# Chunked attention and mixer on one Trainium2 core: all weight factors split from joined words, stores issued from ScalarE's queue, and five pieces of batch 1's attention one border later

## The chip, the cores and the metric

The kernel runs on one core of a Trainium2 chip. The metric is the device time of one execution in microseconds; the time before is the median of three runs. A profile of one execution shows where that execution spent its time.

## The reference, cut to what matters

```python
# q, k, v: (B=4, H=8, S=768, D=64); mem_k, mem_v: (4, 8, 8, 64)
for c in range(24):                       # chunks of 32 queries
    keys = 8 memory keys + positions 32c-16 .. 32c+40 (cut at the ends)
    out[chunk] = softmax(q_c @ keys.T / 8) @ values
x = out, heads side by side               # (4, 768, 512)
h = x.transpose(0, 2, 1) @ U @ V          # U (768, 32), V (32, 768)
u = x + h.transpose(0, 2, 1)
result = u + relu(u @ w1) @ w2            # w1 (512, 2048), w2 (2048, 512)
```

U, V, w1 and w2 arrive as 64-bit numbers. The kernel reads each as two 32-bit words and joins them into one 32-bit number before use.

## The kernel before, in words

Every large product is made of float32 numbers split into a high and a low part, so one product of the mathematics is three products on TensorE. The work of one core goes in this order.

*Batch 0's attention* comes first, in an order written by hand. *Batch 0's mixer* follows in `both_blocks` (L1190): 32 units, each a `w1_step` (L1118, 12 matmuls of 384 columns on one slice f of 128 columns of w1, then ReLU and its split into `hh` and `hl`) and a `w2_step` (L1147, 9 matmuls of 512 columns). Units 0 to 17 take slices 0 to 8 for both blocks of 384 tokens; units 18 to 24 are slices 9 to 15 of block 0, units 25 to 31 the same of block 1. During these units the weights are loaded (raw words `rw`, `raw`), joined and split. `Words` (L197) joins: two ScalarE passes (L217, L231), two VectorE passes (L224, L225) and a VectorE addition (L238). `finish` (L363) issues the store of the joined slice to `val_d` from GpSimd's queue (L366) and makes the low half `w1l` on VectorE (L374) in one of the four buffers of the pool `wlo`. `save_w1l` (L339) is called with the next slice and issues from SyncE's queue (SP): for slices from 9 on `w1l` itself (L343), and for every slice half of `w1h` and half of `w1l`, 128 KB each, to `half_d` (L346).

*Attention of batch 1* is put between the units from 19 on: `border` (L1266) is called twice in each unit, before and after its `w1_step`, and lets the generator of the attention take as many steps as the next entry of `PLAN` (L48) says: transposes of k and q (L589), scores (`kall,qt`, L663), transposes of the probabilities (`ident,pt`, L748), weighing with v (`vb,pT`, L766), and at its end the mixing over tokens (L1004, and six matmuls `g,v` at L1028, each into a bank that VectorE then adds to x, L1030). What is left at unit 28 is done by `following`, which then calls `fold_both` (transposes L1307, VectorE folds L1317 and splits L1322).

*Batches 1 to 3* use seven products in place of eight, after Strassen's scheme. Eight pairs p of w1 slices each have seven factors (`PRODUCTS`, L51), each a tile of high and low halves. `prepare` (L1276) loads two joined slices of `val_d` and has GpSimd make five sums. `build_factor` (L1348) turns a sum into a factor: a ScalarE cast (L1357) and a VectorE subtraction (L1358). Factors 1 and 3 are no sums; they are loaded whole from `half_d` (L1354), 256 KB each, 46 times from ScalarE's queue and twice from SP's. Pairs follow each other without a pause; the factors of the next pair are built while the products of this one run.

The results and the folded x are put in a list `held`; `let_go` (L1107) issues their stores (L1110) from SP's queue at the next border. SP's queue runs in the order in which the program is written, as do TensorE's and GpSimd's; VectorE's from unit 18 on and ScalarE's from unit 2 on are ordered by a scheduler. PSUM banks: three in `ps_a`, two in `ps_h`, three in `ps_o`.

Of the kernel before, what the change touches and what calls it, by code (L numbers as in the profile page):

```python
# [9 lines left out]
F32 = mybir.dt.float32  # L10
# [34 lines left out]
SOON = 8  # L45
RATEL = 3
RATES = 6
PLAN = [0, 1, 1, 1, 1, 1, 1, 1, 1, 1, 1, 1, 1, 1, 1, 1, 2, 1, 1, 1, 0, 0, 0, 0, 0, 0]  # L48
SUMS = ((0, 0, 0, 0, 1, "add"), (2, 0, 0, 1, 1, "add"), (4, 1, 0, 1, 1, "add"),
        (5, 0, 1, 1, 1, "subtract"), (6, 1, 0, 0, 0, "subtract"))  # L50
PRODUCTS = ((6, 0), (2, 1), (0, 2), (1, 0), (5, 1), (4, 2), (3, 0))  # L51
# [4 lines left out]
def chunk_attn_then_mixer_kernel(  # L56
# [13 lines left out]
    nc = tc.nc  # L70
# [262 lines left out]
                c.append(raw)  # L333

    val_d = [dram.tile([P, NCK, P], F32, name=f"vald{f}") for f in range(NF)]
    half_d = [dram.tile([P, NCK, P], F32R, name=f"halfd{f}") for f in range(NF)]
    unsaved = []

    def save_w1l():  # L339
        while unsaved:  # L340
            f, w1l = unsaved.pop(0)
            if f >= SPLIT:
                nc.sync.dma_start(out=w1l_d[f].bitcast(F32), in_=w1l.bitcast(F32))  # L343
            c = 2 * (f % 2)
            for n, w in enumerate((w1h[f], w1l)):
                nc.sync.dma_start(  # L346
                    out=half_d[f][:, 2 * n:2 * n + 2].bitcast(F32), in_=w[:, c:c + 2, :].bitcast(F32),
                )

    def homes(f, which):  # L350
        if which == 0:
# [752 lines left out]
    def put_by(b, t):  # L1104
        held.append((x_d[b, t], xs.pop((b, t))))

    def let_go():  # L1107
        while held:
            to, x = held.pop(0)
            nc.sync.dma_start(out=to, in_=x)  # L1110

    def recall(b, blk):
        for t in range(blk * TB, blk * TB + TB):
# [23 lines left out]
    def add_to_x(b, t, bank, last):  # L1137
        x = xs[(b, t)]
        nc.vector.tensor_tensor(out=x, in0=bank, in1=x, op=ALU.add)
        if last:  # L1140
            held.append((out[b, t * P:(t + 1) * P, :], xs.pop((b, t))))
            if b == B - 1:
                let_go()

    accs = {}

# [43 lines left out]
    def both_blocks(following):  # L1190
# [11 lines left out]
        for n, (blk, f, where, begins, ends) in enumerate(units):  # L1202
            while done[0] < min(2 * NF, 2 * f + 1 + (n > LATE)):
                advance(1)
                more_w()
            if n == 2:
                head.close()
            let_go()
            solo = n >= 2 * SPLIT
            if n == 2 * SPLIT:  # L1210
                paced.close()
            for blk_, m, *_ in units[n:n + AHEAD + 1]:
                if m >= SPLIT and blk_ == 1:
                    get_w1l(m)
            w1l = w1ls[f]
            if f >= SPLIT or blk == 1:
                del w1ls[f]
            if n == 2 * SPLIT - SOON:
                place(1)
            serve(RATEL if n < 2 * SPLIT else RATES)  # L1220
            if n > 2 * SPLIT:
                border()
            if n == 0:
                for c, g3 in rest[:2]:
                    join_uT1(turn_x1(c), c, g3)
            if n == len(units) - 1:
                for m in range(3):
                    build_factor(0, m, nc.sync)
            hid_ = w1_step(0, blk, f, w1l)
            if n == len(units) - 2:  # L1230
                prepare(0)
            if n == len(units) - 5:
                open_turned()
            if n == len(units) - 1:
                open_fast()
                for m in range(3, len(PRODUCTS)):
                    build_factor(0, m, nc.sync)
            if n == 0:
                decode(2, 4)
                for c, g3 in rest[2:]:  # L1240
                    join_uT1(turn_x1(c), c, g3)
                decode(1, 1)
                decode(2, 6)
                decode(1, 6)
                decode(3, 2)
            for _ in range(RATE + (3 < n < 12)):
                advance(1)
                more_w()
            if n > 2 * SPLIT:
                border()  # L1250
            if n >= len(units) - 4:
                following()
            prev.append((blk, f, where, begins, ends) + hid_)
            if solo or n % 2 == 0 or ends:
                while len(prev) > (not ends):
                    while done[0] < 2 * prev[0][1] + 2:
                        advance(1)
                        more_w()
                    w2_step(0, *prev.pop(0))
# [16 lines left out]
    def prepare(p):  # L1276

        whole = [slot([P, NCK, P], F32, "val") for _ in range(2)]
        for side in range(2):
            nc.sync.dma_start(out=whole[side], in_=val_d[2 * p + side])  # L1280
        for m, (n, fa, ca, fb, cb, op) in enumerate(SUMS):
            if m % 2 == 0:
                two = slot([P, 2, 2, P], F32, "sums")
# [61 lines left out]

    factors = {}

    def build_factor(p, n, eng=nc.scalar):  # L1348
        if n < WLO:
            s = wlo.tile([P, NCK, P], F32R, name="w1l")  # L1350
        else:
            s = fast_pools[0].tile([P, NCK, P], F32R, name="s", bufs=len(PRODUCTS) - WLO)
        if n in (1, 3):
            eng.dma_start(out=s.bitcast(F32), in_=half_d[2 * p + (n == 1)].bitcast(F32))  # L1354
        else:
            total = mixed.pop((p, n))
            nc.scalar.copy(out=s[:, 0:2], in_=total)  # L1357
            nc.vector.tensor_tensor(out=s[:, 2:4], in0=total, in1=s[:, 0:2].bitcast(F32), op=ALU.subtract)  # L1358
        factors[p, n] = s

    def split_hidden(src):
# [159 lines left out]
```

## Time and profile before

| | before |
|---|---|
| median of three runs | 660.78 us |
| the three runs | 658.46, 660.78, 665.66 us |
| the profiled execution | 662.22 us |
| its span in the trace | 660.4 us |
| TensorE busy, share of the span | 629.3 us, 95% |
| VectorE, ScalarE, GpSimd busy | 63%, 44%, 20% |
| moved by DMA | 95.76 MB |

The span is 1.8 us shorter than the execution's own time, which holds a start and an end that no engine shows. In a row of the timeline the first number is the start in us, the second the duration in us; then come engine, line, operation, output<-input, and in brackets how long the engine sat idle before it and what ended that. A letter q behind an engine's name means its queue, that is an instruction that issues a DMA. PE is TensorE, DVE VectorE, ACT ScalarE, POOL GpSimd.

### The profile page before, as it was taken

The page shows a single profiled execution, that of the slowest core. Times are in us where ns is not written, and L with a number is a line of the kernel's source. Part 1 is how long each engine was busy: PE and PEld are TensorE (multiplying, and loading weights), DVE is VectorE, ACT ScalarE, POOL GpSimd, SP SyncE. Part 2 cuts the span into 40 slices and gives each one's busy share as a digit, 9 for nine tenths or more (in the row PEclk, how much of TensorE's full clock was granted, in tenths as well). Part 3 has the DMA queues.
Part 4 walks back from the last instruction along what each step waited for, and adds up shares of the span by engine and source line. Part 5 has one row for each costly group of instructions (what it writes and reads, how often), then busy time and mean ns, then how long its engine had stood idle before and what let it go on. Part 6 is the DMA issues. An engine that isn't in the chain of part 4 may idle for free.

```text
span 660.4 us, 15683 instructions
## 1 busy us (share of the span) xinstructions
PE 629.3 (95%) x6196; PEld 551.2 (83%) x6198; DVE 414.0 (63%) x839; ACT 290.7 (44%) x724; POOL 129.9 (20%) x192
## 2 busy tenths in 40 slices
PE   8798998989989999999999999999999999999997
PEld 7567997969868989988898898988979889989986
DVE  4877978766535955756665953746746976336342
ACT  4566776575313445533333545533433633314221
POOL 4610000200000243212410222202420358000000
PEclk9999998999979999999999999999999999999999
DMA  8899896668253478632422658731421474202111
GB/s 208 186 294 321 258 259 212 169 196 269 76 125 108 134 228 202 175 89 66 114 65 79 201 168 199 199 88 36 122 88 45 163 252 142 70 0 65 33 49 48
DMA packets 133075, 95.76 MB, mean 145 GB/s; under 512 B 88586, under 2 KB 107786, under 8 KB 133002
## 3 DMA queue, kind: packets, MB, share of 16 engines
q1 hardware_dynamic: 125002, 78.37, 41.5%
q10 hardware_dynamic: 6624, 12.06, 6.1%
q0 software_dynamic: 1376, 4.33, 1.8%
q8 instruction: 49, 0.80, 0.5%
q14 instruction: 24, 0.20, 0.1%
HBM read 72.58 MB, written 21.23 MB: 142 GB/s over the span
## 4 chain that ended last, share of the span: by engine, by line
PE 76%; DVE 7%; DMA 7%; issue 5%; ACT 2%; SPq 2%; POOL 0%; DVEq 0%; POOLq 0%; ACTq 0%
PE ps_h L1389 18%; PE acc L1176 13%; PE ps_a L1389 7%; PE acc L1181 6%; PE ps_h L1176 5%; PE ps_h L1125 5%; PE ps_a L1176 3%; PE ps_h L1181 3%; PE ps_a L589 2%; PE ps_a L766 2%; DMA vb<-in_v_dram 2%; PE ps_a L663 2%; PE ps_a L748 2%; PE ps_a L1181 1%; PE ps_a L1307 1%
## 5 line engine op out<-in xcount | busy, mean ns | idle before, releaser
L1285 POOL TENSOR_TENSOR sums<-val 128x256 f32<-128x256 f32 x120 | 94.3, 819 | 270.9 <-DMA val<-vald 101.5
L1176 PE MATMUL acc<-w,hh 128*128 128x512 f32 x366 | 97.6, 401 | 1.0 <-DVE w L374 1.0
L1389 PE MATMUL ps_h<-th,w1l 128*128 128x384 f32 x288 | 83.4, 343 | 2.3 <-DVE part L1406 1.2
L1176 PEld LDWEIGHTS acc<-w,hh 128*128 128x128 f32 x366 | 67.2, 189 | 15.3 <-issue 1.5
L1389 PEld LDWEIGHTS ps_h<-th,w1l 128*128 128x128 f32 x288 | 52.8, 188 | 6.7 <-issue 2.6
L1365 DVE SCALAR_TENSOR_TENSOR hl<-kept,hh 128x384 fp32r<-128x384 f32 x48 | 28.5, 594 | 44.3 <-PE ps_a L1181 24.3
L1389 PE MATMUL ps_h<-th,s 128*128 128x384 f32 x192 | 52.9, 336 | 0.0
L1181 PE MATMUL acc<-w,hl 128*128 128x512 f32 x183 | 51.8, 391 | 0.0
L1364 ACT ACTIVATE hh<-kept 128x384 fp32r<-128x384 f32 x48 | 25.5, 532 | 58.3 <-PE ps_a L1176 38.1
L1389 PE MATMUL ps_h<-tl,w1l 128*128 128x384 f32 x144 | 48.4, 336 | 0.0
L1125 PE MATMUL ps_h<-uh,w1h 128*128 128x384 f32 x124 | 43.3, 355 | 3.1 <-DVE hl L1132 3.1
L1176 PE MATMUL ps_h<-w,hh 128*128 128x512 f32 x156 | 43.0, 397 | 0.0
L1125 PE MATMUL ps_h<-ul,w1h 128*128 128x384 f32 x124 | 42.3, 349 | 0.6 <-issue 0.6
L1181 PEld LDWEIGHTS acc<-w,hl 128*128 128x128 f32 x183 | 34.4, 188 | 7.5
L1176 PE MATMUL ps_a<-w,hh 128*128 128x512 f32 x132 | 37.9, 390 | 1.8 <-ACT hh L1131 1.8
L1395 ACT COPY part<-ps_h 128x384 f32<-128x384 f32 x24 | 11.5, 480 | 59.7 <-PE ps_h L1389 56.9
L1357 ACT CAST s<-sums 128x256 fp32r<-128x256 f32 x72 | 28.4, 414 | 17.5 <-PE ps_h L1389 13.9
L1358 DVE TENSOR_TENSOR w1l<-sums,w1l 128x256 fp32r<-128x256 f32 x48 | 22.9, 492 | 19.8 <-ACT w1l L1357 19.8
L1389 PEld LDWEIGHTS ps_h<-th,s 128*128 128x128 f32 x192 | 35.1, 187 | 0.0
L1365 DVE SCALAR_TENSOR_TENSOR hl<-ps_a,hh 128x384 fp32r<-128x384 f32 x24 | 13.4, 557 | 33.8 <-ACT hh L1364 33.8
L1358 DVE TENSOR_TENSOR s<-sums,s 128x256 fp32r<-128x256 f32 x72 | 33.8, 484 | 0.8 <-ACT s L1357 0.8
L1176 PEld LDWEIGHTS ps_h<-w,hh 128*128 128x128 f32 x156 | 28.4, 188 | 5.6
(274 smaller groups left out, 1373.8 us busy)
## 6 DMA issues: line engine op xcount, KB each, us to landing
val<-vald SPq DMA_DIRECT2D x48, 256.0 KB
w1l<-halfd ACTq DMA_DIRECT2D x46, 256.0 KB
rw<-in_moe_w_ch_dram SPq DMA_DIRECT2D x14, 512.0 KB
out_dram<-x SPq DMA_DIRECT2D x24, 256.0 KB
vb<-in_v_dram SPq DMA_DIRECT2D x56, 98.0 KB
raw<-in_moe_w_ch_dram SPq DMA_DIRECT2D x20, 256.0 KB
qn<-in_q_dram SPq DMA_DIRECT2D x36, 128.0 KB
xd<-x SPq DMA_DIRECT2D x18, 256.0 KB
```

The lines of the kernel that those rows point to most:

```text
L589: nc.tensor.transpose(out=psv[:, p, r, :], in_=half[:, r, 2 * p:2 * p + 2, :].rearrange("n h d -> n (h d)"), identity=ident,)
L663: nc.tensor.matmul(out=psv[s][CK * i:CK * i + CK, t, p % 2, p // 2, :], lhsT=qt[p // 2][rows, p % 2, NI * t + i, :], rhs=kall[rows, NB * ( ...
L748: nc.tensor.transpose(out=psv[:, j, :], in_=pt[:, P * j:P * j + P], identity=ident)
L1125: nc.tensor.matmul(out=ph[:, :TOK], lhsT=w[:, c, :], rhs=u[c], start=(m == 0), stop=(m + 1 == len(parts)),)
L1176: nc.tensor.matmul(out=acc[tt], lhsT=h[:, sl], rhs=w, start=(begins and m == 0), stop=False,)
L1181: nc.tensor.matmul(out=acc[tt], lhsT=hl[:, sl], rhs=w2h[f], start=False, stop=ends is not None)
L1285: nc.gpsimd.tensor_tensor(out=two[:, m % 2], in0=a, in1=b_, op=getattr(ALU, op))
L1357: nc.scalar.copy(out=s[:, 0:2], in_=total)
L1358: nc.vector.tensor_tensor(out=s[:, 2:4], in0=total, in1=s[:, 0:2].bitcast(F32), op=ALU.subtract)
L1364: nc.scalar.activation(out=hh, in_=src, func=AF.Relu)
L1365: nc.vector.scalar_tensor_tensor(out=hl, in0=src, scalar=0.0, in1=hh.bitcast(F32), op0=ALU.max, op1=ALU.subtract,)
L1389: nc.tensor.matmul(out=banks[at_], lhsT=w[:, wc, :], rhs=t[:, i, c, :], start=(n < 3 and m == 0), stop=(m + 1 == len(parts)), skip_group_c ...
```

## The change

It has four parts. (1) `half_d` is gone, with its 32 stores and its 48 loads. (2) Factors 1 and 3 are split like the other five, straight from the joined slices that `prepare` has loaded: one cast and one subtraction each. (3) `let_go` issues its stores from ScalarE's queue; only the last batch's six results stay with SP. (4) `PLAN` puts steps 1 to 5 of batch 1's attention one border later, catches up with a 2 at the seventh entry, and puts the steps from the former second 2 on one border later, the last into `following`.

```diff
-PLAN = [0, 1, 1, 1, 1, 1, 1, 1, 1, 1, 1, 1, 1, 1, 1, 1, 2, 1, 1, 1, 0, 0, 0, 0, 0, 0]
+PLAN = [0, 0, 1, 1, 1, 1, 2, 1, 1, 1, 1, 1, 1, 1, 1, 1, 1, 1, 1, 1, 0, 0, 0, 0, 0, 0]
@@ save_w1l
             if f >= SPLIT:
                 nc.sync.dma_start(out=w1l_d[f].bitcast(F32), in_=w1l.bitcast(F32))
-            c = 2 * (f % 2)
-            for n, w in enumerate((w1h[f], w1l)):
-                nc.sync.dma_start(
-                    out=half_d[f][:, 2 * n:2 * n + 2].bitcast(F32), in_=w[:, c:c + 2, :].bitcast(F32),
-                )
@@ let_go
-    def let_go():
+    def let_go(eng=nc.scalar):
         while held:
             to, x = held.pop(0)
-            nc.sync.dma_start(out=to, in_=x)
+            eng.dma_start(out=to, in_=x)
@@ add_to_x
             if b == B - 1:
-                let_go()
+                let_go(nc.sync)
@@ prepare
+        mixed[p, 1], mixed[p, 3] = whole[1][:, 2:4, :], whole[0][:, 0:2, :]
@@ build_factor
-        if n in (1, 3):
-            eng.dma_start(out=s.bitcast(F32), in_=half_d[2 * p + (n == 1)].bitcast(F32))
-        else:
-            total = mixed.pop((p, n))
-            nc.scalar.copy(out=s[:, 0:2], in_=total)
-            nc.vector.tensor_tensor(out=s[:, 2:4], in0=total, in1=s[:, 0:2].bitcast(F32), op=ALU.subtract)
+        total = mixed.pop((p, n))
+        nc.scalar.copy(out=s[:, 0:2], in_=total)
+        nc.vector.tensor_tensor(out=s[:, 2:4], in0=total, in1=s[:, 0:2].bitcast(F32), op=ALU.subtract)
```

Three places show how the order moves. The first is SP's queue at 160 to 182 us of the trace before; `vb_103` and `vb_102` are tiles of v for batch 1's attention, `w1ld` the stored low halves of w1, `out_dram` the results of block 0. Before:

```order
L429 DMA w1l<-w1ld_122 128x512
L552 DMA vb_103<-mv 8x8x256 x2
L570 DMA vb_103<-in_v_dram 56x8x64 x4
L1110 DMA out_dram<-x 128x512 x3
L429 DMA w1l<-w1ld_123 128x512
L570 DMA vb_103<-in_v_dram 56x8x64 x4
L570 DMA vb_102<-in_v_dram 56x7x64
```

After:

```order
L423 DMA w1l<-w1ld_122 128x512
L546 DMA vb_103<-mv 8x8x256 x2
L564 DMA vb_103<-in_v_dram 56x8x64 x4
L423 DMA w1l<-w1ld_123 128x512
L564 DMA vb_103<-in_v_dram 56x8x64 x4
L564 DMA vb_102<-in_v_dram 56x7x64
```

The three stores no longer stand between the two halves of `vb_103`; they now stand in ScalarE's queue.

The second place is TensorE at the scores of the first tile (unit 20 before, unit 21 after), where `ident,kn` and `ident,qn` are the transposes of k and q and `kall,qt` the scores. Before:

```order
L1125 MATMUL ps_h<-uh,w1l 128x384 x4
L589 MATMUL ps_a<-ident,kn 128x128 x8
L1176 MATMUL acc_1290<-w_1832,hh 128x512 x2
L1176 MATMUL acc_1291<-w_1832,hh 128x512 x2
L1176 MATMUL acc_1292<-w_1832,hh 128x512 x2
L1181 MATMUL acc_1290<-w_1832,hl 128x512
L1181 MATMUL acc_1291<-w_1832,hl 128x512
L1181 MATMUL acc_1292<-w_1832,hl 128x512
L663 MATMUL ps_a<-kall,qt 32x64 x64
```

After:

```order
L1119 MATMUL ps_h<-uh,w1l 128x384 x4
L657 MATMUL ps_a<-kall,qt 32x64 x64
L1170 MATMUL acc_1270<-w_1890,hh 128x512 x2
L1170 MATMUL acc_1271<-w_1890,hh 128x512 x2
L1170 MATMUL acc_1272<-w_1890,hh 128x512 x2
L1175 MATMUL acc_1270<-w_1890,hl 128x512
L1175 MATMUL acc_1271<-w_1890,hl 128x512
L1175 MATMUL acc_1272<-w_1890,hl 128x512
L583 MATMUL ps_a<-ident,kn 128x128 x8
```

The scores stood behind unit 20's nine matmuls with w2; now unit 21's w1 step comes first, and they stand ahead of its nine. The transposes of k have changed places with them in the same way: from behind a w1 step to behind the nine matmuls that followed it.

The third is TensorE in unit 28, the end of batch 1's attention, where `g,v` is the mixing over tokens and `ident,x` the first transposes of the fold. Before:

```order
L1028 MATMUL ps_a<-g_3023,v_99 128x512 x3
L1125 MATMUL ps_h<-uh_1133,w1h_1960 128x384
L1125 MATMUL ps_h<-ul_1134,w1h_1960 128x384
L1125 MATMUL ps_h<-uh_1133,w1h_1960 128x384
L1125 MATMUL ps_h<-ul_1134,w1h_1960 128x384
L1125 MATMUL ps_h<-uh_1133,w1h_1960 128x384
L1125 MATMUL ps_h<-ul_1134,w1h_1960 128x384
L1125 MATMUL ps_h<-uh_1133,w1h_1960 128x384
L1125 MATMUL ps_h<-ul_1134,w1h_1960 128x384
L1125 MATMUL ps_h<-uh_1133,w1l 128x384 x4
L1028 MATMUL ps_a<-g_3023,v_99 128x512 x3
L1307 MATMUL ps_a<-ident,x 128x128 x8
```

After:

```order
L1119 MATMUL ps_h<-ul_1118,w1h_1922 128x384
L1119 MATMUL ps_h<-uh_1117,w1h_1922 128x384
L1119 MATMUL ps_h<-ul_1118,w1h_1922 128x384
L1119 MATMUL ps_h<-uh_1117,w1l 128x384 x4
L1022 MATMUL ps_a<-g_2998,v_99 128x512 x6
L1302 MATMUL ps_a<-ident,x 128x128 x8
```

The w1 step that stood between the two groups of three now stands ahead of both.

## Rows read from the trace of the kernel before

**Rows 1.** The page's first part: busy time, share of the span, instructions of each engine.
```profile
PE 629.3 (95%) x6196; PEld 551.2 (83%) x6198; DVE 414.0 (63%) x839; ACT 290.7 (44%) x724; POOL 129.9 (20%) x192
```

**Rows 2.** Windows: start:end us, length, busy per engine, PEclk, DMA share, GB/s.
```profile
60.00:64.00 4.00, 4.00 (x21) 3.61 (x21) 3.90 (x8) 2.10 (x6) 0.00 (x0) 1.00 0.81 271
...
90.00:100.00 10.00, 10.00 (x52) 9.18 (x52) 6.81 (x13) 6.06 (x14) 0.78 (x1) 1.00 0.97 249
...
109.00:112.70 3.70, 3.70 (x14) 3.60 (x14) 3.70 (x8) 1.61 (x4) 0.54 (x1) 0.56 0.18 73
...
184.50:191.20 6.70, 6.08 (x94) 5.31 (x79) 1.85 (x7) 0.45 (x1) 0.00 (x0) 0.50 0.75 169
...
240.00:640.00 400.00, 396.54 (x3509) 352.38 (x3508) 236.87 (x483) 157.45 (x395) 90.52 (x122) 1.00 0.39 113
```

**Rows 3.** Timeline of POOL, DVE and PE, 92 to 109 us.
```profile
93.19 0.78 POOL L366 DMA_DIRECT2D vald<-vb  x1 [4.52 <-DVE vb L238]
...
99.39 0.43 DVE L224 TENSOR_SCALAR vb<-vb 128x512 int32<-128x512 int32 x1 [3.02 <-DMA vald<-vb]
...
108.76 0.44 PE L1125 MATMUL ps_h<-uh,w1h 128*128 128x384 f32 x1 [3.09 <-DVE hl L1132]
```

**Rows 4.** DMA issues of the whole run: KB each, median us to landing.
```profile
vald<-vb POOLq DMA_DIRECT2D x5, 256.0 KB, 4.0
```

**Rows 5.** Timeline of PE, 59 us: an earlier wait.
```profile
59.79 1.66 PE L1176 MATMUL ps_a<-w,hh 128*128 128x512 f32 x6 [1.77 <-ACT hh L1131]
```

**Rows 6.** Timeline of PE, 136 to 145 us.
```profile
136.12 0.66 PE L589 MATMUL ps_a<-ident,kn 128*128 128x128 f32 x4 [0.66 <-DVE x L1139]
137.32 0.66 PE L589 MATMUL ps_a<-ident,kn 128*128 128x128 f32 x4 [0.54 <-DVE x L1139]
...
144.76 0.66 PE L589 MATMUL ps_a<-ident,kn 128*128 128x128 f32 x4 [1.27 <-ACT kall L619]
```

**Rows 7.** Timeline of SP, DVE and PE, 176 to 183 us.
```profile
176.32 2.22 SPq L1110 DMA_DIRECT2D out_dram<-x  x3
...
179.07 2.84 SPq L570 DMA_DIRECT2D vb<-in_v_dram  x5
...
181.80 1.28 DVE L682 TENSOR_TENSOR pt<-ps_a,mx 128x512 f32<-128x512 f32 x2
...
180.20 0.27 PE L766 MATMUL ps_a<-vb,pT 64*32 64x64 f32 x2
182.93 0.35 PE L766 MATMUL ps_a<-vb,pT 64*32 64x64 f32 x16 [2.46 <-DMA vb<-in_v_dram]
```

**Rows 8.** Timeline of DVE and PE, 204 to 209 us.
```profile
204.57 1.89 DVE L1030 TENSOR_TENSOR x<-ps_a,x 128x512 f32<-128x512 f32 x3 [1.00 <-PE ps_a L1028]
...
206.96 0.86 PE L1028 MATMUL ps_a<-g,v 96*128 96x512 f32 x3
208.13 1.25 PE L1307 MATMUL ps_a<-ident,x 128*128 128x128 f32 x8 [0.32 <-DVE x L1030]
```

**Rows 9.** Timeline of SP and PE, 213 to 238 us.
```profile
213.59 10.49 SPq L1354 DMA_DIRECT2D w1l<-halfd  x2
...
237.78 0.41 PE L1389 MATMUL ps_a<-th,w1l 128*128 128x384 f32 x1 [1.28 <-DMA w1l<-halfd]
```

**Rows 10.** The page's costliest groups: busy us, mean ns, idle before and its releaser.
```profile
L1357 ACT CAST s<-sums 128x256 fp32r<-128x256 f32 x72 | 28.4, 414 | 17.5 <-PE ps_h L1389 13.9
L1358 DVE TENSOR_TENSOR w1l<-sums,w1l 128x256 fp32r<-128x256 f32 x48 | 22.9, 492 | 19.8 <-ACT w1l L1357 19.8
L1365 DVE SCALAR_TENSOR_TENSOR hl<-ps_a,hh 128x384 fp32r<-128x384 f32 x24 | 13.4, 557 | 33.8 <-ACT hh L1364 33.8
```

**Rows 11.** Lines L1354 and L1110: duration ns min/median/max, first and last start.
```profile
L1354 ACTq DMA_DIRECT2D w1l<-halfd x46: 326/326/1507, 234.2 to 617.6; - x46
...
L1110 SPq DMA_DIRECT2D xd<-x x18: 319/438/1192, 205.3 to 522.2; - x18
```

**Rows 12.** Timeline of PE where one pair's products wait for the last's.
```profile
538.98 0.44 PE L1389 MATMUL ps_h<-th,w1l 128*128 128x384 f32 x1 [0.86 <-DVE part L1406]
```

More of the change, by code (lines that the diff above doesn't have):

```diff
@@ L335, in chunk_attn_then_mixer_kernel @@
     val_d = [dram.tile([P, NCK, P], F32, name=f"vald{f}") for f in range(NF)]
-    half_d = [dram.tile([P, NCK, P], F32R, name=f"halfd{f}") for f in range(NF)]
     unsaved = []
@@ L1227, in both_blocks @@
                 for m in range(3):
-                    build_factor(0, m, nc.sync)
+                    build_factor(0, m)
             hid_ = w1_step(0, blk, f, w1l)
@@ L1236, in both_blocks @@
                 for m in range(3, len(PRODUCTS)):
-                    build_factor(0, m, nc.sync)
+                    build_factor(0, m)
             if n == 0:
@@ L1346, in chunk_attn_then_mixer_kernel, with build_factor @@
     factors = {}
-    def build_factor(p, n, eng=nc.scalar):
+    def build_factor(p, n):
         if n < WLO:
```

## The prediction

> **What bounds the kernel now.** Read the busy line of the page first. TensorE (PE) is busy 629.3 of the span's 660.4 us [rows 1], so 31 us at most can be had from waits; nothing in the change removes a matmul. Next, windows, to see where those us are: in the 400 us from 240 on PE is busy 396.54, so all the later batches together idle 3.5 us [rows 2]. What the change can gain lies before 240, in waits of one to three us and in two stretches where the granted clock fell to the lower level, 1.2 GHz: 3.70 us at a mean of 0.56 of full speed, and 6.70 us at 0.50 [rows 2]. Third, the timeline of PE at each wait, and from there the engine or transfer that ended it. The total DMA time does not bound the kernel (share 0.39 in the later batches), but there are stretches where it does (0.97 at 90 to 100) [rows 2].
>
> All sums are made against the profiled execution's 662.2 us. It is 1.4 above the median of 660.8, so 1.4 is taken off at the end. About 1% (6.6 us) is what a measurement of this kernel can tell from no change.
>
> **Term A, the dropped stores of halves (about 95 to 113 us): gain 2.5.** GpSimd issues the store of a joined slice at 93.19; VectorE needs its buffer again and stands still for 3.02 us until 99.39 [rows 3]. That is 6.2 us to landing, where the median of such a store is 4.0 [rows 4]. PE then waits 3.09 us at 108.76 for VectorE [rows 3], and the clock is low behind it [rows 2]. In that stretch SP's queue issues two of the dropped stores, 256 KB. Their own time bounds the gain from below: at the 249 GB/s of this window [rows 2] they take 1.05 us. From above: the store lands in 4.0, 2.2 us sooner, and the clock stays high, which in 3.70 us at 0.56 is worth 3.70 x 0.44 = 1.6; together 3.8. A bound below that of 0 stays too, if other loads fill the place at once. I take 2.5, the middle of 1.05 and 3.8, because which loads move up is not seen.
>
> The Trainium skill has another reason for a slow store from GpSimd (SBUF — State Buffer, Who interferes with whom): such a store can be starved by a VectorE operation that holds a port both share. By that rule the dropped stores would change nothing here and A would be 0. VectorE was idle for the last 3.02 us of the transfer [rows 3], so the trace speaks against it for those.
>
> The other waits for joined words before 130 us can also shrink, since the 32 dropped stores, 4 MB, leave SP's queue and the DMA engines; I book nothing for that.
>
> **Term B, the first pieces of batch 1's attention (135 to 146 us): gain 1.7.** The transposes of k stand right behind a w1 step and wait 0.66 and 0.54 for banks that VectorE is still adding from, and the second four of a later group 1.27 for ScalarE's copies [rows 6]. In the new order nine matmuls with w2 come first; six of these alone take 1.66 us [rows 5], more than the 1.20 of the first two waits, so those go. The 1.27 is a wait for one of three banks, which the new order does not add to; two of its neighbours move away, and I give it 0.5 of gain. Bounds: 2.5 if all three go, and a loss of 0.5 if the scores, now beside a w1 step, wait instead.
>
> **Term B2, the end of that attention (204 to 209 us): loss 1.0.** In the new order the six `g,v` matmuls follow each other, each needs a bank, and there are three. VectorE's adds take 1.89 for three, 0.63 each [rows 8]; the last three matmuls wait for the first three adds, and the fold's transposes for the next. Adds 1 to 6 end about 1.1, 1.7, 2.3, 3.0, 3.6 and 4.2 us after the first matmul begins, so the second bank of the transposes begins at 3.6. In the order before, the first three took 0.86 like the second, the second with their wait 208.13 - 206.96 = 1.17, and the first bank of the transposes half of 1.25 [rows 8]: 2.6 without the w1 step. The loss is 3.6 - 2.6 = 1.0; between 0, if the scheduler's adds overlap better, and 3, if the folds are also late for the products that follow.
>
> **Term C, the stores that left SP's queue (176 to 191 us): gain 4.1.** SP can issue the three results' stores only at 176.32, when VectorE's last additions come, and the second half of v's loads stands behind them, at 179.07; PE does two weighing matmuls at 180.20 and waits 2.46 until 182.93 for v [rows 7]. Then the clock is low for 6.70 us, 6.08 of them busy and 0.62 idle [rows 2]. With the stores gone, v is there long before. But the third matmul also needs a bank of the three in `ps_a`, since scores and weighing stand side by side and take four. The bank is free when VectorE's first `pt` is done, at 181.80 + 0.64 = 182.44 [rows 7]. So a wait of 182.44 - 180.47 = 2.0 takes the place of 2.46, and only 0.5 is sure. The clock decides the rest: 6.08 / 2 = 3.0 for the slow work, and the 0.62. After a wait of 1.77 [rows 5] the granted clock read 1.00, in the window from 60 to 64 [rows 2]; after 2.46 it read 0.50. The row nearest to 2.0 is the 1.77, so I take 0.5 + 3.0 + 0.6 = 4.1 and keep 0.5 as the lower end and 2.46 + 3.0 + 0.6 = 6.1 (the whole wait too) as the upper.
>
> The Trainium skill says that transfers begun on ScalarE's, SyncE's or GpSimd's queue share the same 16 DMA engines, so that spreading them saves only the issuing time (DMA: Bandwidth & Descriptors, Issuing engines are not separate DMA queues). By that rule alone the moved stores would be worth nothing to PE. The row at 179.07 shows a loss of another kind: loads stood behind stores that waited for VectorE.
>
> **Term D, the first pair of batch 1 (213 to 238 us): gain 1.2.** SP stands 10.49 us at two loads of halves that wait for buffers, the joined slices of the next pair come after that, and PE waits 1.28 at 237.78 for a half [rows 9]. No such load is left. I take 1.2; bounds 1.3 and -0.5, if the cast and subtraction that replace it are late.
>
> **Term E, 48 factors now built (227 to 640 us): loss 1.0.** ScalarE gets 48 casts of 0.414 = 19.9 us [rows 10] and 36 store issues of 0.438 = 15.8, and loses 46 load issues of 0.326 = 15.0 [rows 11]: 20.7 more. VectorE gets 48 subtractions of 0.492 = 23.6 us [rows 10]. The cover: VectorE is busy 236.87 of the 400 us [rows 2], and before the split of the hidden values alone it waits 33.8 us for ScalarE [rows 10], 1.4 at each of 24. PE cannot gain more than its 3.5 us of idle there. The price if cover fails: where one pair's products follow the other's, PE already waits for VectorE, 0.86 at 538.98 [rows 12] (four of the 24 changes of pair have such a wait, this the longest). One more pair of subtractions there is 2 x 0.49 = 0.98. Bounds: gain 1.5, loss 5 (five such places). I take one, 1.0.
>
> **Sum.** 2.5 + 1.7 - 1.0 + 4.1 + 1.2 - 1.0 = 7.5; 662.2 - 7.5 = 654.7, and 1.4 less is the prediction, 653.3. The end of the kernel and its last stores are as before.
>
> **Rival 1: waits take the place of waits.** C's bank wait still brings the clock down, and A's store is no earlier because loads fill the gap. Then C is 0.5, A is 0, and the sum 0.5 + 1.7 - 1.0 + 1.2 - 1.0 = 1.4: 660.8, or 659.4 by the median. For it: 2.0 is near 2.46 too, and the DMA share around A is 0.97 [rows 2]. Against it: 256 KB of that traffic do go, and the 2.0 is nearer to the wait that left the clock high.
>
> **Rival 2, the slower side: stores block ScalarE.** ScalarE takes its queue in order, and each of nine groups (in each of three batches two of results and one of x) now waits there for VectorE's last add, with `hh` or the copy out of a bank queued behind, and PE behind those. A group costs one add more to wait for, 0.63 [rows 8], and three issues of at least 0.32, 1.0 [rows 11]: 1.6. Nine are 14.4, and 662.2 - 7.5 + 14.4 = 669.1, or 667.7 by the median. It decides from the fifth group on, where 8.0 outweighs 7.5. For it: five stores of x stand in a row ahead of a copy. Against it: ScalarE is 44% busy [rows 1] and mostly waits for PE, so most groups should fall into its waits.
>
> **Rival 3, better:** A, B, C and D at their upper ends, 3.8 + 2.5 + 6.1 + 1.3 = 13.7, with B2 and E as forecast: 662.2 - 11.7 = 650.5, or 649.1.
>
> **How the numbers follow.** Forecast 0.45, within 650 to 657; rival 1 0.29; rival 2 0.12; rival 3 0.14. One percent below the median is 654.2. Faster by over 1% holds rival 3 and some 0.32 of the forecast, 0.46; slower (over 667.4) rival 2 with its worst part, 0.12; the rest, 0.42, is the same. The range leaves out a part of rival 2 and the best of rival 3: 646 to 664.
>
> **What would show it.** Right: in the new trace SP loads v by about 170; no low clock at 184 to 191; the joined slice at 99 no later than 4 to 5 us from its issue; PE waits for no load near 238; new waits of about 1 us at the six `g,v`. Wrong: the clock still low behind the second scores (C), VectorE's subtractions named before PE's waits at the change of pair (E), or idle time of ScalarE at its store issues, with PE waiting for `hh` (rival 2).

## The result, and the profile after

The changed kernel takes 665.01 us (median of 20 runs, 662.2 to 668.62) against 662.34 of the kernel before, measured beside it (20 runs). The ratio is 1.0055 with a 95% interval of 1.003 to 1.008: slower by half a percent. The forecast was 653.3 with a range of 646 to 664, so the time lies outside the range, and on the other side of no change. The profiled execution of the changed kernel took 666.09 us, that of the kernel before 662.22 [rows 1 are of the latter]. A few executions are slow whatever the kernel (the longest, 862.61 us, is the only profiled one of the kernel with the front of the new `PLAN` alone); the ratios leave them out, and that profile is not read.

The busy line of the page and two of its costliest groups, of the changed kernel:

```profile
PE 629.2 (95%) x6198; PEld 550.6 (83%) x6198; DVE 435.6 (66%) x887; ACT 307.5 (46%) x772; POOL 132.9 (20%) x192
...
L1280 POOL TENSOR_TENSOR sums<-val 128x256 f32<-128x256 f32 x120 | 98.0, 844 | 265.9 <-DMA val<-vald 83.5
L1381 PE MATMUL ps_h<-th,w1l 128*128 128x384 f32 x288 | 84.3, 345 | 5.7 <-DVE x L1133 3.2
```

TensorE does the same work [rows 1]; VectorE has 21.6 us more, ScalarE 16.8 more. The last row is the new fact: the first products of a pair now wait 3.2 us for VectorE's line L1133, the addition of the last results to x.

Where the time went is best read by laying the two timelines of TensorE side by side and taking the start of the same matmuls (the low-half group of a w1 step, or the first product of a pair; where the order moved, work can stand on the other side of a mark). Times in us:

| the same matmuls | before | after | after - before | stretch, change of the difference |
|---|---|---|---|---|
| unit 1 | 49.52 | 48.91 | -0.61 | |
| unit 3 | 63.37 | 64.21 | +0.84 | clock at 59: +1.45 |
| unit 15 | 118.03 | 115.59 | -2.44 | A: -3.28 |
| unit 19 | 134.60 | 132.16 | -2.44 | |
| unit 25 | 178.12 | 178.24 | +0.12 | B: +2.56 |
| unit 28 | 206.25 | 202.25 | -4.00 | C: -4.12 |
| unit 29 | 212.69 | 212.35 | -0.34 | B2: +3.66, about 0.7 of it work that moved behind the mark |
| batch 1, pair 2 | 249.93 | 248.32 | -1.61 | D: -1.27 |
| batch 2, pair 6 | 481.50 | 481.86 | +0.36 | E: +1.97 |
| batch 3, pair 2 | 550.54 | 554.37 | +3.83 | E: +3.47 |

After that the difference stays at 3.83, which is that of the two spans, 664.2 and 660.4. Each column is one execution; how far a stretch differs between executions is taken up with the experiments.

The rows behind these steps are, first, windows of the changed kernel (columns as in rows 2):

```profile
59.00:62.00 3.00, 2.93 (x8) 2.33 (x9) 2.88 (x6) 1.16 (x4) 0.00 (x0) 0.58 0.93 301
107.92:112.00 4.08, 4.08 (x21) 3.77 (x22) 4.08 (x8) 3.03 (x8) 0.54 (x1) 1.00 0.16 64
144.20:147.20 3.00, 2.99 (x13) 2.99 (x14) 1.47 (x3) 3.00 (x13) 0.00 (x0) 0.60 1.12 265
183.00:190.00 7.00, 5.27 (x149) 4.74 (x150) 3.80 (x10) 2.18 (x5) 0.00 (x0) 1.00 0.04 10
206.00:210.00 4.00, 3.90 (x14) 3.26 (x14) 3.16 (x8) 1.75 (x5) 0.89 (x2) 0.57 0.72 264
533.40:537.40 4.00, 4.00 (x14) 4.00 (x15) 1.25 (x3) 1.10 (x3) 1.54 (x3) 0.57 0.85 269
240.00:640.00 400.00, 393.47 (x3483) 349.20 (x3482) 252.06 (x521) 170.53 (x436) 87.65 (x114) 1.00 0.29 82
```

The clock holds at 107.92 and at 183, where it fell before [rows 2]; it falls at 59, at 144, at 206 and at 533, where it had not. In the 400 us from 240 TensorE is busy 393.47, 3.07 less than before [rows 2]. Second, the timeline: GpSimd's store of a joined slice, two rows of VectorE, two of SP's issues of v, and TensorE's waits:

```profile
95.23 0.78 POOL L360 DMA_DIRECT2D vald<-vb  x1 [5.73 <-DVE vb L238]
...
100.12 0.43 DVE L224 TENSOR_SCALAR vb<-vb 128x512 int32<-128x512 int32 x1 [1.71 <-DMA vald<-vb]
...
107.92 0.44 PE L1119 MATMUL ps_h<-uh,w1h 128*128 128x384 f32 x1 [1.42 <-DVE hl L1126]
...
144.21 0.66 PE L583 MATMUL ps_a<-ident,kn 128*128 128x128 f32 x4 [2.77 <-ACT kall L613]
...
171.55 1.38 SPq L564 DMA_DIRECT2D vb<-in_v_dram  x3
...
173.45 0.91 SPq L564 DMA_DIRECT2D vb<-in_v_dram  x2
...
181.98 1.28 DVE L676 TENSOR_TENSOR pt<-ps_a,mx 128x512 f32<-128x512 f32 x2
...
183.02 1.47 PE L760 MATMUL ps_a<-vb,pT 64*32 64x64 f32 x126 [2.43 <-DMA vb<-in_v_dram]
186.75 0.44 PE L1119 MATMUL ps_h<-uh,w1h 128*128 128x384 f32 x1 [1.71 <-issue]
...
204.14 1.10 PE L1022 MATMUL ps_a<-g,v 96*128 96x512 f32 x2 [0.32 <-DVE x L1024]
205.79 0.49 PE L1022 MATMUL ps_a<-g,v 96*128 96x512 f32 x1 [0.56 <-DVE x L1024]
...
533.36 0.42 PE L1381 MATMUL ps_h<-th,w1l 128*128 128x384 f32 x1 [2.97 <-DVE x L1133]
```

VectorE's wait for the store of a joined slice is 1.71 in place of 3.02, TensorE's behind it 1.42 in place of 3.09 [rows 3]. The wait for a load of halves at 238 [rows 9] is gone. The row at 183.02 names a load of v, but it is a wait for a bank: the loads of v that stand ahead of it were issued by 174.4, and the first of VectorE's two `pt`, which frees the bank, ended at about 182.6. The next wait, 1.71 at 186.75 (0.62 at 187.46 before), is marked "issue": the trace shows nothing that it waits for.

The largest new wait, 2.97 at 533, is followed back in the timeline of the other engines. Changed kernel, 516 to 534 us (the last row a window):

```profile
516.79 5.29 SPq L1274 DMA_DIRECT2D val<-vald  x4
...
520.37 5.00 POOL L1280 TENSOR_TENSOR sums<-val 128x256 f32<-128x256 f32 x5 [31.11 <-DMA val<-vald]
524.19 10.39 POOL L1280 TENSOR_TENSOR sums<-val 128x256 f32<-128x256 f32 x11
...
528.51 4.10 DVE L1317 TENSOR_TENSOR tl<-fold,th 128x512 fp32r<-128x512 f32 x4
532.53 1.27 DVE L1133 TENSOR_TENSOR x<-ps_h,x 128x512 f32<-128x512 f32 x2
...
520.00:534.00 14.00, 11.03 (x54) 9.01 (x54) 14.00 (x22) 5.66 (x12) 13.63 (x15) 1.00 0.29 78
```

The same place in the kernel before, 517 to 536 us:

```profile
530.45 1.53 SPq L1110 DMA_DIRECT2D out_dram<-x  x3
532.07 2.81 SPq L1280 DMA_DIRECT2D val<-vald  x6
...
524.42 2.19 POOL L1285 TENSOR_TENSOR sums<-val 128x256 f32<-128x256 f32 x2
534.96 0.74 POOL L1285 TENSOR_TENSOR sums<-val 128x256 f32<-128x256 f32 x1 [8.34 <-DVE w1l L1358]
...
527.60 2.21 DVE L1322 TENSOR_TENSOR tl<-fold,th 128x512 fp32r<-128x512 f32 x4
...
530.56 0.42 PE L1389 MATMUL ps_h<-th,w1l 128*128 128x384 f32 x1 [0.54 <-DVE x L1139]
```

Before, SP's queue stood at the stores of results until VectorE's last addition, at 530.45, and the next joined slices were loaded only behind them, from 532.07. GpSimd had nothing to add between 526.6 and 534.96, and VectorE's four fold subtractions `tl` took 2.21 us. In the changed kernel the stores are not in that queue; four slices are loaded from 516.79 on, GpSimd adds without a pause until 534.6, and the same four subtractions take 4.10 us. VectorE's last addition, for which TensorE waits, is late by most of that wait: the four subtractions account for 1.89 of the 2.43 us by which it grew. The clock fell behind it (0.57 in the 4 us from 533.4); the stretch around the change to batch 3 loses 3.47 in all. At the beginning of batch 2 the same is seen in another group. Changed kernel:

```profile
386.15 4.43 POOL L1280 TENSOR_TENSOR sums<-val 128x256 f32<-128x256 f32 x5 [8.21 <-DVE kept L1400]
...
388.18 2.69 DVE L1350 TENSOR_TENSOR s<-sums,s 128x256 fp32r<-128x256 f32 x3
...
391.39 0.45 PE L1381 MATMUL ps_a<-th,s 128*128 128x384 f32 x1 [1.20 <-DVE part L1389]
```

The kernel before, where GpSimd stood idle until 392.83:

```profile
392.83 0.73 POOL L1285 TENSOR_TENSOR sums<-val 128x256 f32<-128x256 f32 x1 [13.14 <-DMA val<-vald]
...
387.58 0.42 DVE L1358 TENSOR_TENSOR s<-sums,s 128x256 fp32r<-128x256 f32 x1
```

Three subtractions that take 0.42 each alone take 0.9 each under GpSimd's sums, and TensorE then waits 1.20 for VectorE.

### The profile page after: what moved, and what is told of

It reads as the page before. It is cut to its first block, busy times and chain, and to the rows that moved or that the text cites. A ratio compares the mean times of both kernels' runs of the same rounds, so it can differ in the third digit from the quotient of the medians.

```text
span 664.2 us, 15673 instructions
## 1 busy us (share of the span) xinstructions
PE 629.2 (95%) x6198; PEld 550.6 (83%) x6198; DVE 435.6 (66%) x887; ACT 307.5 (46%) x772; POOL 132.9 (20%) x192
## 3 DMA queue, kind: packets, MB, share of 16 engines
q1 hardware_dynamic: 114922, 64.21, 35.3%
## 4 chain that ended last, share of the span: by engine, by line
PE 70%; DVE 12%; DMA 7%; issue 5%; SPq 4%; ACT 2%; POOL 0%; DVEq 0%; POOLq 0%; ACTq 0%
PE ps_h L1381 17%; PE acc L1170 12%; PE ps_a L1381 7%; PE acc L1175 6%; PE ps_h L1170 5%; PE ps_h L1119 4%; PE ps_a L1170 3%; PE ps_h L1175 3%; DMA rw<-in_moe_w_ch_dram 2%; PE ps_a L583 2%; PE ps_a L760 2%; PE ps_a L657 2%; DMA vald<-vbe 2%; PE ps_a L1175 1%; PE ps_a L1302 1%
## 5 line engine op out<-in xcount | busy, mean ns | idle before, releaser
L1280 POOL TENSOR_TENSOR sums<-val 128x256 f32<-128x256 f32 x120 | 98.0, 844 | 265.9 <-DMA val<-vald 83.5
L1350 DVE TENSOR_TENSOR s<-sums,s 128x256 fp32r<-128x256 f32 x72 | 36.8, 522 | 1.7 <-ACT s L1349 1.7
L1349 ACT CAST s<-sums 128x256 fp32r<-128x256 f32 x72 | 28.8, 414 | 16.8 <-PE ps_h L1381 16.8
L1389 DVE TENSOR_TENSOR part<-ps_a,part 128x384 f32<-128x384 f32 x24 | 13.3, 554 | 30.5 <-PE ps_a L1381 27.4
L1381 PE MATMUL ps_h<-tl,s 128*128 128x384 f32 x96 | 32.3, 336 | 0.0
```

The costliest lines, as they stand in the source:

```text
L1280: nc.gpsimd.tensor_tensor(out=two[:, m % 2], in0=a, in1=b_, op=getattr(ALU, op))
L1381: nc.tensor.matmul(out=banks[at_], lhsT=w[:, wc, :], rhs=t[:, i, c, :], start=(n < 3 and m == 0), stop=(m + 1 == len(parts)), skip_group_c ...
L1389: nc.vector.tensor_tensor(out=ta, in0=b2, in1=ta, op=ALU.subtract)
```

## The experiments

Two theories were tried against each other for the later batches: that the moved stores let GpSimd's sums run into VectorE's fold (theory 1), and that the 48 added casts and subtractions cost the time, or ScalarE's stores hold up its copies. A third question was what the new `PLAN` costs. The change has three separable parts (halves dropped and factors split; stores on ScalarE; `PLAN`), and all eight combinations were run. A median is that of 6 to 12 runs (20 for the changed kernel), a ratio that to the kernel before beside it.

| halves dropped, factors split | stores on ScalarE | new PLAN | median us | ratio (95%) |
|---|---|---|---|---|
| no | no | no | 661.8 to 662.3 | 1 |
| yes | no | no | 658.72 | 0.9959 (0.9932 to 0.9986) |
| no | yes | no | 663.82 | 1.0033 (1.0007 to 1.0059) |
| no | no | yes | 665.75 | 1.0058 (1.0027 to 1.0089) |
| yes | no | yes | 659.99 | 0.9978 (0.9944 to 1.0012) |
| yes | yes | no | 662.17 | 0.9993 (0.9961 to 1.0025) |
| no | yes | yes | 668.11 | 1.0105 (1.0065 to 1.0144) |
| yes | yes | yes | 665.01 | 1.0055 (1.003 to 1.008) |

The three single parts are -0.41, +0.33 and +0.58%; their sum, +0.50%, is close to the measured +0.55%. So one part gains and two lose. Single intervals are some 0.3% wide to either side, but the signs hold in every pair of lines that differ in one part: the halves gain 0.4 to 0.8%, the stores lose 0.3 to 0.8%, `PLAN` loses 0.2 to 0.7%.

The profiles of these kernels, one execution each, show where. For each stretch of the marks above, its length against that in the kernel before, in us (C and B2 are taken together, so that work moved over the mark between them does not count):

| halves dropped | stores on ScalarE | new PLAN | A | B | C and B2 | D | E |
|---|---|---|---|---|---|---|---|
| yes | no | no | -3.3 | -1.6 | -0.9 | -0.2 | -0.6 |
| no | yes | no | -2.4 | +0.2 | -3.4 | +2.7 | +2.2 |
| no | no | yes | -1.5 | +1.4 | +2.8 | +0.9 | -0.2 |
| yes | no | yes | -0.8 | -0.1 | -0.7 | +0.1 | -1.8 |
| yes | yes | no | -2.0 | -1.9 | -2.8 | -1.3 | +4.9 |
| no | yes | yes | -0.5 | +2.3 | -0.5 | +1.2 | +2.7 |
| yes | yes | yes | -3.3 | +2.6 | -0.5 | -1.3 | +5.4 |

Two things stand out. Stretch A is shorter in every line, also where the halves are kept, so the profile of the kernel before was long there by itself. And E is not a sum: the halves dropped alone gain a little, the stores moved alone lose 2.2, both together lose 4.9.

### PLAN put back

```diff
-PLAN = [0, 0, 1, 1, 1, 1, 2, 1, 1, 1, 1, 1, 1, 1, 1, 1, 1, 1, 1, 1, 0, 0, 0, 0, 0, 0]
+PLAN = [0, 1, 1, 1, 1, 1, 1, 1, 1, 1, 1, 1, 1, 1, 1, 1, 2, 1, 1, 1, 0, 0, 0, 0, 0, 0]
```

> The changed kernel with PLAN as before; all else changed. Theory (the later borders cost: batch 1's copies then queue behind the last words on ScalarE, and the six g,v wait for banks): the two losses read from the trace, about 1.5 us at 135 to 157 and 3 us at 206 to 213, go, so about 661 us against 665.0, and no wait near 2.8 us for ScalarE's copies at 144. Rival (the plan is neutral, the loss lies in the later batches): 664 to 666.

Measured: 662.17, 2.8 us less than the changed kernel. TensorE's waits at the two places, in this kernel:

```profile
141.10 0.66 PE L583 MATMUL ps_a<-ident,kn 128*128 128x128 f32 x4 [1.27 <-ACT kall L613]
...
201.46 1.25 PE L1302 MATMUL ps_a<-ident,x 128*128 128x128 f32 x8 [0.32 <-DVE x L1024]
```

The 2.77 is 1.27 again, as before [rows 6], and the fold's transposes wait only 0.32 [rows 8]. By the marks of the table above, the stretches B and C with B2 change by -1.9 and -2.8 us, where the changed kernel has +2.6 and -0.5. The theory of its expectation holds; the wait in the later batches stays, 3.11 us at 526.56.

### Stores put back on SP

```diff
-    def let_go(eng=nc.scalar):
+    def let_go(eng=nc.sync):
```

> The changed kernel with all stores of x and results issued from SP as before. Theory 1 (stores in SP's queue held back the loads of joined slices; without them GpSimd's sums run into VectorE's fold and double its subtractions): the four tl subtractions before a batch change take about 2.2 us again in place of 4.1, the 2.97 us wait at 533 is gone, later batches about 4 us shorter; the wait for v at 183 and the low clock behind it come back, about 4 us, so 664 to 666 in all. Rival (the 48 subtractions themselves cost the time): waits of the later batches stay and the early gain is lost, about 669.

Measured: 659.99, better than either theory said. The fold before batch 3 and what follows, in this kernel:

```profile
527.93 1.53 SPq L1104 DMA_DIRECT2D out_dram<-x  x3
...
525.09 2.21 DVE L1317 TENSOR_TENSOR tl<-fold,th 128x512 fp32r<-128x512 f32 x4
...
528.05 0.41 PE L1381 MATMUL ps_h<-th,w1l 128*128 128x384 f32 x1 [0.54 <-DVE x L1133]
```

The subtractions take 2.21 and the wait is 0.54 again with all 48 new factors in place. From pair 2 of batch 1 to pair 2 of batch 3 this kernel gains 1.8 us on the one before (-1.24 to -3.02) where the changed one loses 5.4. So the factors alone are not what the later batches pay for. The low clock at v came back in part, 0.76 in the 7 us from 183, where it had been 0.50 in the kernel before. The loss of about 4 us that the theory expected with it does not show: units 25 to 29 take 33.9 us against 34.1 in the changed kernel, where the clock fell at the six `g,v`; here it held (1.00 in the 6 us from 203).

### Halves kept, the two other parts as changed

The edit puts `half_d`, its stores and its loads back into the changed kernel.

> The kernel before with the new PLAN and the stores on ScalarE's queue, but the halves still stored and loaded, so no 48 new factors. Theory 1 (sums meet fold because the stores left SP): the slow tl subtractions and the wait of about 3 us before batch 3 stay; the gain of 3.3 us at 99 to 118 is lost: 667 to 669. Rival (the 48 casts and subtractions cost the later batches 5 us): those come back, 662 to 664, with tl at 0.55 us each.

Measured: 668.11, the slowest, as theory 1 said. Without any new factor the last four `tl` take 3.56 us and TensorE waits 2.96 at 532.63. At the beginning of batch 2, though, it has no wait like the 1.20 of the changed kernel: that loss needs the new factors and the moved stores together.

### Only the stores moved

```diff
-    def let_go():
+    def let_go(eng=nc.scalar):
-            nc.sync.dma_start(out=to, in_=x)
+            eng.dma_start(out=to, in_=x)
```

> The kernel before with only its stores of x and results moved to ScalarE's queue. Theory 1: gains about 4 us at 176 to 200 (v is there early), loses 4 to 5 where GpSimd's sums meet the fold: 661 to 664. Rival (ScalarE blocked by its stores, copies out of banks late at each batch change): 666 to 668. Rival (stores moved are worth only the gain at v): 658 to 659.

Measured: 663.82, at the upper end of theory 1. By the marks it gains 3.4 us from unit 25 to unit 29 and loses 3.2 around the change to batch 3. The time lies outside both rivals' ranges: it is not as slow as a blocked ScalarE was said to make it, nor as fast as a gain at v alone.

### GpSimd held back, stores left on ScalarE

```diff
+        if p == 1 and held:
+            nc.gpsimd.tensor_copy(out=gate_[:, 0:1], in_=held[-1][1][:, 0:1])
         for m, (n, fa, ca, fb, cb, op) in enumerate(SUMS):
```

The copy stands ahead of the loop over `SUMS` (the line that makes its tile `gate_` is not shown), so that GpSimd's sums for pair 1 wait for VectorE's last addition to x.

> The changed kernel with one GpSimd copy of one element per partition put ahead of the sums for pair 1, read from the last x of the batch before, so that these sums begin after VectorE's last addition of that batch; stores stay on ScalarE. Theory 1 (GpSimd's sums double VectorE's fold subtractions): the last four tl take 2.2 us in place of 4.1, the 2.97 us wait before batch 3 falls to about 0.5, and with its slow clock 3 to 5 us go: 660 to 662 against 665.0. Rival (ScalarE's stores hold up its copies and so PE): tl faster but PE still late at 533, 664 to 665.

Measured: 663.43. Its fold subtractions, and the window around them:

```profile
527.98 2.22 DVE L1320 TENSOR_TENSOR tl<-fold,th 128x512 fp32r<-128x512 f32 x4
...
520.00:534.00 14.00, 14.00 (x73) 11.96 (x72) 12.16 (x26) 7.20 (x16) 0.75 (x2) 1.00 0.52 165
```

This is the run that separates the theories for the wait at 533. The stores are still in ScalarE's queue, in the same order; only GpSimd is later, busy 0.75 us of these 14 where it had been busy 13.63. The subtractions take 2.22 and TensorE does not wait at all (14.00 busy of 14.00). So GpSimd's sums made them slow, and ScalarE's stores did not hold up TensorE there. From pair 6 of batch 2 to pair 2 of batch 3 the difference to the kernel before goes down by 0.6 where it rose by 3.5. The median moved less than that, 1.6 us, to between the two ranges expected, and its interval (1.0007 to 1.0051) touches that of the changed kernel; a wait of 1.22 us at 393.40 for VectorE, at the beginning of batch 2, stays, and by the marks 1.1 us is still lost between pair 2 of batch 1 and pair 6 of batch 2. In its profile the clock also fell at 59 (0.65 in the 3.5 us from 60.5) and at v (0.52 in the 7 us from 184.5). How much of the 3.4 us between its median and that of the kernel with SP's stores each of these makes up is open.

The same copy with `PLAN` put back:

> The changed kernel with PLAN as before and the GpSimd copy that holds the sums of pair 1 back. Theory 1: old_plan measured 662.2 and the gate takes 3 to 5 us off: 657 to 659, faster than the kernel before by 0.5 to 0.8%. Rival: the gate does nothing, 662.

Measured: 659.78, ratio 0.9967 (0.9943 to 0.999), 2.4 us below the kernel without the copy and just above the range of theory 1; the two intervals overlap.

### Only the halves dropped

The changed kernel with `PLAN` put back and stores on SP.

> The kernel before with only the halves dropped and factors 1 and 3 split from joined words; old PLAN, stores on SP. Theory (this part alone is a gain: 3 us at 99 to 118 and 1 us at 238, its 48 casts and subtractions hidden): 657 to 659 against 662. Rival (the 48 subtractions cost the later batches what the early part gains): 661 to 663.

Measured: 658.72, ratio 0.9959 (0.9932 to 0.9986). In its trace the difference to the kernel before goes from -4.16 at pair 2 of batch 1 to -4.72 at pair 2 of batch 3: with the stores on SP the 48 casts and subtractions cost nothing there. At v it has the old wait and the old clock:

```profile
179.86 0.35 PE L760 MATMUL ps_a<-vb,pT 64*32 64x64 f32 x16 [2.47 <-DMA vb<-in_v_dram]
...
180.00:187.00 7.00, 6.59 (x139) 5.59 (x134) 3.13 (x8) 0.66 (x2) 0.00 (x0) 0.51 1.06 223
```

### Only PLAN, and its two halves

The kernel before with the new `PLAN`:

> The kernel before with only the new PLAN. Theory (the later borders cost at 135 to 178 and at the six g,v in any surrounding): about 2.5 to 4 us more, 664.5 to 666. Rival (the new PLAN costs only together with the other parts): 661 to 663.

Measured: 665.75, ratio 1.0058 (1.0027 to 1.0089). Its waits at the two places:

```profile
146.12 1.12 PE L589 MATMUL ps_a<-ident,kn 128*128 128x128 f32 x4 [2.66 <-ACT kall L619]
...
208.06 1.09 PE L1028 MATMUL ps_a<-g,v 96*128 96x512 f32 x2 [0.32 <-DVE x L1030]
209.72 0.50 PE L1028 MATMUL ps_a<-g,v 96*128 96x512 f32 x1 [0.57 <-DVE x L1030]
```

These are those of the changed kernel to within 0.11 us, so the new order can make them by itself. The waits at `g,v` are the same in all six profiles with the new end. The wait for ScalarE's copies is not: over the five profiles with the new front it is 1.26 to 3.47, and 1.26 is what the old order has. Then each half of the new `PLAN` alone:

```diff
 the front
+PLAN = [0, 0, 1, 1, 1, 1, 2, 1, 1, 1, 1, 1, 1, 1, 1, 1, 2, 1, 1, 1, 0, 0, 0, 0, 0, 0]
 the end
+PLAN = [0, 1, 1, 1, 1, 1, 1, 1, 1, 1, 1, 1, 1, 1, 1, 1, 1, 1, 1, 1, 0, 0, 0, 0, 0, 0]
```

> The kernel before with only the front of the new PLAN (steps 1 to 5 one border later, the 2 at the seventh entry; the end as before). Theory (each end costs about half): the trace loses 1.4 from 135 to 178 and nothing at 206 to 213; 663 to 664.5. Rival (all of the 3.9 lies at the end): 662.

> The kernel before with only the end of the new PLAN (the former second 2 a 1, the rest one border later). Theory: a loss of 2.5 to 3 from 200 to 213, where six g,v follow each other and the clock falls behind their waits; 664 to 665.5. Rival (the six g,v cost only their two waits of 0.9): 662.5 to 663.

Measured: the front alone 664.79, ratio 1.0048 (1.0021 to 1.0075); the end alone 664.5, ratio 1.0042 (1.0019 to 1.0066). Both cost, some 2 to 3 us each (the front 0.3 more than the range of its theory), and neither rival holds. They are not parts of a sum: 0.48 and 0.42% are more than the 0.58% of the whole. Where the end's loss lies is not shown: in its profile the clock held at the six `g,v` (1.00 in the 6 us from 206), against its theory, and units 25 to 29 lost only 0.3 us.

### A version that beats both

The kernel with only the halves dropped, and of the stores only the first three results from ScalarE:

```diff
             if n == 2:
                 head.close()
-            let_go()
+            let_go(nc.scalar if n < 28 else nc.sync)
```

> split_only, and of the stores only the first three results (block 0 of batch 0) issued from ScalarE; the rest from SP. Theory (their place ahead of v's loads in SP's queue is the only thing worth moving; the other stores are the brake on GpSimd's sums): split_only measured 658.7; the wait at 180 falls from 2.47 to the bank's 2.1 and what follows it to unit 25 gains 1 to 2: 656.5 to 658. Rival (the bank wait decides alone): 658.5 to 659.

Measured: 655.18 (6 runs), ratio 0.9893 (0.9855 to 0.9932): 1.1% faster than the kernel before, some 1.5% faster than the changed one, and better than the range of its theory. Its wait at v and two windows:

```profile
179.18 1.46 PE L760 MATMUL ps_a<-vb,pT 64*32 64x64 f32 x126 [2.17 <-DMA vb<-in_v_dram]
...
180.00:187.00 7.00, 5.01 (x89) 4.52 (x77) 3.37 (x9) 1.85 (x4) 0.00 (x0) 1.00 0.12 25
...
240.00:640.00 400.00, 397.45 (x3503) 352.31 (x3502) 252.23 (x524) 169.57 (x428) 87.06 (x113) 1.00 0.30 84
```

The wait at v is the bank's, 2.17, and the clock behind it holds. The later batches idle 2.55 us, less than before, with the same 252 us of work on VectorE as in the changed kernel: with the later stores left on SP the sums keep out of the last part of the fold, and the wait before batch 3 is 0.54. Against the kernel with only the halves dropped, units 25 to 28 take 2.1 us less, at the place that the theory names. The whole difference of the two profiles, 3.1 us, also holds gains and losses of 1.0 to 1.6 in other stretches, the clock at 59 among them.

## Why the prediction was wrong, point by point

The forecast was a gain of 7.5 us for the profiled execution; the two profiles show a loss of 3.8. Of these 11.3 us B makes 4.3, E 4.4, B2 2.7 (0.7 of it moved work) and the clock at 59 another 1.45. The 1.4 taken off for the median was a step of its own that failed: the median of three runs, 660.78, was low, and over 20 runs it is 662.34, level with the profile. The signs that were to show it right came nearly all (v loaded by 174, no low clock at 184 to 191, no wait for a load near 238, the waits at `g,v`), and none of those that were to show it wrong: the losses of B and E lay where no sign had been set.

**A, forecast a gain of 2.5: right in kind, its size in part luck.** By the marks it is 3.28, inside the bounds, and made of the two things named: TensorE's wait is 1.67 shorter, and the rest, 1.61, is the clock, which held. The store landed 4.9 us after its issue, not 6.2. But the profile of the kernel before is the longest of five with the halves in this stretch, 54.7 us; the other four have 51.9 to 54.2, the seven without halves 51.4 to 53.8. The mean gain is 0.8. What all profiles agree on is the wait: it is shorter in each of the four pairs that differ in the halves alone, by 0.6 to 1.7. The prediction's inference that by the Trainium skill's rule on stores from GpSimd (SBUF — State Buffer, Who interferes with whom) A would be zero is not borne out by that wait; and VectorE again stood idle for the last 1.71 us of the transfer.

**B, forecast a gain of 1.7: wrong, a loss of 2.6.** The step that failed is "the 1.27 is a wait for one of three banks, which the new order does not add to; two of its neighbours move away". The first two waits did go. But the copies that free those banks stand in ScalarE's queue, and moved a border later they stand behind the last words being joined. In the changed kernel:

```profile
140.60 0.43 DVE L224 TENSOR_SCALAR vb<-vb 128x512 int32<-128x512 int32 x1 [0.94 <-DMA vald<-vb]
...
141.85 0.75 ACT L231 ACTIVATE vb<-raw 128x256 int32<-128x256 uint32 x2 [2.77 <-DVE vb L225]
142.50 0.60 ACT L392 CAST w2last<-vb 128x512 fp32r<-128x512 f32 x1
143.01 0.19 ACT L601 COPY kall<-ps_a 128x48 f32<-128x48 f32 x1
```

ScalarE stands 2.77 us at a joining step that waits for VectorE, then finishes it, and only then copies. TensorE waits the same 2.77, and the clock falls behind it, to 0.60 in the 3 us from 144.2. The five profiles with the new front all have this order on ScalarE. TensorE's wait goes with the time at which the joining step comes: it was 1.26 and 1.80 where the clock held, 2.66 to 3.47 in the three where it fell.

**B2, forecast a loss of 1.0: right in kind, too small.** The two waits came as worked out, 0.32 and 0.56. What was left out is the clock: 0.57 in the 4 us from 206. By the marks the loss is 3.66, less about 0.7 of moved work: 3.0, the worst bound. The clock fell there in four of the six profiles with the new end; in the two where it held the loss is 1.6.

**C, forecast a gain of 4.1: right in kind; that the number matches is luck.** 4.12 by the marks, but 1.5 of it is `PLAN`'s: 0.7 is work that moved behind the mark, and 0.77 the matmuls `x,u_sb`, which take 1.91 in the new order and 2.68 in the old. What is left for the stores is 2.65. The clock gave 3.3 where 3.0 was forecast. The waits gave back 0.6 where a gain of 1.1 was forecast: the bank's wait took v's place, as foreseen, but at 2.43, not 2.0 (2.09 to 2.17 in the six other kernels with these stores moved), and the idle 0.62 did not go but became the unexplained 1.71. With only the stores moved the stretch is 3.4 shorter, all of it the clock. The clock held here and in four of those six; in the other two it fell.

**D, forecast a gain of 1.2: right,** 1.27. No profile without the halves waits for a load there; the five with them wait 0.9 to 2.0 for one. Over the four pairs the gain is 0.2 to 3.9.

**E, forecast a loss of 1.0: wrong, 5.4.** The cover of the 48 subtractions held where the stores stayed on SP (a gain of 0.6 where they were added alone). The step that failed is the price of the moved stores: the sum counted their issue time on ScalarE and their place ahead of v's loads, and nothing else that stood behind them in SP's queue. Behind them stood the loads of joined slices for the next pairs, and so GpSimd's sums; the waiting stores kept these out of the end of VectorE's fold. Taken out of the queue, they cost 3.47 us around the change to batch 3 (3.25 where only the stores moved), and with the new factors the 1.97 before it, where GpSimd's sums now met the factors' own subtractions (1.20 of it is the wait at 391). So the cover fails too once the stores are moved: with them on ScalarE the new factors cost 2.7 us in E, in both pairs, and with them on SP they cost nothing. The forecast priced the two apart. Rival 2 had the right part of the change on the slower side, but its mechanism, ScalarE blocked by its stores, is not what happened at the largest wait.

**The clock at 59** put another 1.45 us on this one profile. It is not a mark of the change (below); how often it falls in the executions that were not profiled is not known.

## What to carry to other kernels

A store that waits in a queue is also a brake on every load behind it; before it is moved, follow those loads to the engines that they set free and ask what these will run beside. Parts that are cheap alone can cost together. One profile is one execution: before a stretch's gain is put down to a cause, see how long that stretch is in other profiles. Take a change of several parts apart: here one part gained 0.4%, two lost 0.3 and 0.6%, and the first with a twelfth of the second (three stores of 36) gave 1.1%. When a step is moved along one engine's order, look at the queue of the engine that must free its bank, not only at the banks.

## What the runs showed of the hardware

VectorE's subtraction of two tiles of 128x512 took 2.21 / 4 = 0.55 us alone and 4.10 / 4 = 1.03 while GpSimd's additions ran, and 0.55 again (2.22 / 4) when only GpSimd was held back. The Trainium skill says that a VectorE instruction with two inputs in SBUF contends with a GpSimd instruction that reads SBUF (SBUF — State Buffer, Who interferes with whom); the traces here agree, with 1.03 against 0.55.

The length of the last wait alone does not settle the clock in these traces. At 59 us TensorE waits 1.74 to 1.77 us at the same matmul [rows 5] in each of twelve profiles, of ten experiments and the two kernels; behind it the clock fell to the lower level in four of them (0.58 in the 3 us from 59 in the changed kernel, 0.51 at the same place in the kernel with only the end of `PLAN`) and held in the other eight. At v it held behind waits of 2.09 to 2.43 in five kernels and fell behind 2.11 in two (0.82 and 0.52). In the five where the results' stores stood ahead of v's loads it fell each time (0.50 to 0.76). So the forecast's choice of the nearest wait gave the right answer at v in the changed kernel, but not in two of the six others, and would have given the wrong one at 59 in four profiles of twelve.
